# Half-megabyte clears between the key loads, one turn for a block's list loads, and new place numbers in an attention-and-experts kernel

## The chip, the cores and the metric

The kernel runs on one core of a Trainium2 chip. The metric is the time of one execution in device microseconds (us): lower is better. Five engines with instruction queues of their own work beside each other: TensorE (PE in the rows, its weight loads PEld), VectorE (DVE), ScalarE (ACT), GpSimd (POOL) and SyncE (SP). In this kernel SP computes nothing. It issues all plain transfers, one after the other, and POOL issues the gathers and scatters. TensorE runs at one of two clocks, 1.2 and 2.4 GHz; a granted clock of 1.00 in a stretch is the upper one throughout.

## What is computed

Attention of 8 batches with 8 heads, 576 rows, a causal window of 128 keys and a bias that falls with distance, and then a layer of 8 experts, of which every token takes two:

```python
scores = np.where(mask, scale * q @ k.T + slope * -abs(rel), -1e9)    # per batch and head
attn = np.exp(scores - scores.max(-1))                                # 576 x 576, window 128
x = ((attn / attn.sum(-1)) @ v)                                       # -> 4608 tokens x 512
noisy_logits = x @ w_gate + np.log1p(np.exp(x @ w_noise)) * noise     # 4608 x 8
top2 = the two largest of each row; top2_w = softmax over the two
for e in range(8):
    for k in range(2):
        mask = top2[:, k] == e
        h = np.maximum(x[mask] @ w1[e], 0.0)                          # 512 -> 1024
        out[mask] += top2_w[mask, k, None] * (h @ w2[e])              # 1024 -> 512
```

## The kernel before

**Attention and routing.** For each of 32 pairs (two heads of one batch) a key load brings queries and keys into one of five buffers (L465; batch b's values in two halves, L475). TensorE multiplies them (L524, L535), VectorE adds the bias and finds each row's largest (L539), ScalarE takes the exponentials (L563), TensorE transposes (L577, L581), ScalarE moves the result out of the accumulators (L276), and GpSimd cuts the window's ragged edge with two `affine_select` instructions (L600, L601). Only after these can TensorE weigh the values (L614, L623). At the end of a batch the result is turned row-major (L783 and VectorE L786), stored to the table `xs` in memory (L794, L797), and multiplied by the gate (L816, L827). `route` then picks the two experts of each token (noisy logits on POOL, L950 to L953, the largest by VectorE L885 and L889), counts ahead of each token how many earlier ones chose the same expert (L893 to L898) and writes the token numbers into per-expert lists (matmul L933, VectorE L941 and L942). A scatter on POOL adds these lists into the table `slots` in memory (L1009). The gates' weights go to `xs` by SP (L1069, L1073).

**The early blocks.** Batches are counted from b=0 to b=7. When b=3, b=5 and b=7 are through (`CUTS`), a block of expert 0's tokens is prepared, of 384, 384 and 256 rows, the first while attention still runs. For such a block, `first_ids` loads three (or two) pieces of the list from `slots` back by SP (L1078), VectorE turns them to indices (L1083, L1084, L1044), POOL gathers the rows of `xs` (L1337), VectorE splits them into 16-bit parts (L1434), and TensorE multiplies them by w1 (L1463) and w2 (L1613). Expert weights come by SP (L1321) and are split by VectorE (L1327).

**The second blocks.** Each expert then has two blocks of 512 rows (products L1489 and L1620) and one of what is left, 192 to 96 rows, whose first products (L1463) come as eight groups of twelve; each group's accumulator is emptied by ScalarE (L1588) and VectorE (L1603). Results are scattered into `out` by POOL (L1724), with addition. So `out` must be zero before the first of them: `set_ups` writes zeros to it and to the end of `xs` from a tile of zeros (L441), in ten transfers of 1 MB, and the tile then becomes a gather buffer.

**What sets the order.** The whole program is written as strands that a planner, the class `Order`, runs against a simple model of the five engines when the program is built. An operation has a duration in the model and a rank; an engine takes the waiting operation with the lowest rank, and buffers are handed out by rank as well. The ranks are sums of place numbers from the tables at the head of the file (`LOAD`, `VALUES`, `FINE`, `ROUTE`, `SCATTER` and so on) and of a batch's or a block's number. On TensorE an operation of the kind that ran last may go ahead if its rank is within `NEAR` of the best. The order that comes out is fixed: on the chip each engine runs its list in that order and waits wherever something is not there yet. A line `yield order.now + 2.5` tells the planner that a transfer takes so long to land; on the chip it is no wait, but it shifts what is issued when.

Two waits of the program matter here. The load of a list reads what the scatters wrote, and it waits for the landing of every scatter that stands ahead of it in the program, needed for this block or not. And the strand of `route` hands the table `slots` on from scatter to scatter through the ring `listing`, which the planner holds for the counted landing time only.

Of the kernel before, what the change touches and what calls it, by code (L numbers as in the profile page):

```python
# [13 lines left out]
AF = mybir.ActivationFunctionType  # L14
OP = mybir.AluOpType
AX = mybir.AxisListType
# [27 lines left out]
ZERO, EMPTY = -868.7, -2  # L44
LOAD = 1336.2
VALUES = 522.7
GATE = (586.3, 114.2, 10.8, 223.3, 430.5, 595.2, 1222.1, 914.0)
ROUTE = (342.7, 2091.0, 1245.6, 114.7, 453.4, 734.2, 1823.4, 1585.4)
SCATTER = (825.8, 1619.1, 1254.4, -2580.7, 356.1, -2057.0, -1202.6, 1165.8)
FFN0, FFN1 = -37.1, 674.3  # L50
WEIGHTS = (1547.8, 1129.9)
TOKENS = -408.2
FINE = (-269.6, -67.8, 591.7, 499.2, 364.6, 91.4, -84.0, -165.4, -508.6, -68.4, -409.6, 76.9, 124.7, -71.9, -108.9, -18.6, -921.6, 304.5, 493.5, 400.7, 136.3, 66.3, 526.5, 2.2, 234.2, -476.5, -453.8, -47.5, -184.4, -278.0, 410.0, 13.0, 37.2, 126.9, -246.8, 12.9, -248.7, 24.3, -130.2, 10.5, -211.1, 146.0, -91.2, -314.4, -30.9, 272.5, -306.7, -204.8, -795.2, 68.5, 336.3, -528.3, 344.2, 61.4, -456.9, 111.8, -186.5, -50.6, -10.3, -525.8, -189.2, 13.2, 55.1, 270.0, 177.0, -536.1, 113.3, 36.7, -51.7, -60.8, 589.7, -248.0, -73.3, -88.5, 652.2, -8.9, -517.4, 295.6, 24.0, -285.0, 895.7, 310.8, -678.8, -379.9, -384.9, -317.9, 31.8, 33.5, -239.2, -604.6, -100.3, -134.7, 154.5, -665.9, 43.3, 311.1, 207.6, -18.8, 338.4, -65.9, -144.2, -324.3, 36.8, 219.5, -55.9, -124.3, 200.0, -551.8, 229.5, 106.3, 1.0, 383.8, -156.7, -416.1, -291.1, -190.4, 45.4, -262.7, -141.2, 180.6, -150.6, -450.1, -201.8, 120.2, -203.1, -129.0, 273.6, 32.0, 96.8, -401.0, -263.6, 134.3, -151.3, 504.8, 21.3, -241.5, -6.7, -424.3, -701.9, 780.4, 28.0, 576.4, -208.7, 237.4, -534.3, 273.3, 215.7, 380.0, 228.8, -184.6, 104.7)
STAGE = (855.9, -105.9, 923.9, 172.5, -770.8, 1148.3, 1067.9, 742.9)
MIDDLE = 1144.0
RESULT = 1472.4
SIZES = (1334.5, 424.5, 1529.3)
SOON = -672.8
TIGHT = (1, 5, 7)
QUICK = (5, 7)  # L60
LATE = (2094.9, -890.9, 647.9, 1175.8, 179.1, -270.3, -892.6, -769.0, 507.2, -1321.9, -1248.3, -168.7, -2569.7, -1705.9, -1040.2)
LAG = 0.2
ADD, TWS = 0.34, 5
BEHIND = 11.7
# [3 lines left out]
PACE, READ_BY, AHEAD = 1.1, 2.0, 297.8  # L68
HELD = 3
SWITCH, NEAR = 0.093, 39.0  # L70
# [168 lines left out]
def attention_moe(ctx: ExitStack, tc: tile.TileContext, qk_, v, w_gate, w_noise, noise, w1, w2,  # L239
# [142 lines left out]
    def set_ups():  # L382
# [479 lines left out]
    def route(b):  # L862
# [156 lines left out]
        yield order.now + 2.5  # L1019
# [5 lines left out]
    def landed_list():  # L1025
        yield order.now + 2.1
        put(listing, 0)

    def first_ids(blk, cut, rank):
# [16 lines left out]
        yield dve(0.4, FINE[65] + rank, clipped)  # L1046
# [4 lines left out]
    def gates_out(b, rank, tp, d, oh, gg, gd, placed_):  # L1051

        G = nc.gpsimd
        yield pool(0.3, FINE[66] + rank, lambda: G.tensor_tensor(d[:, :, 0], tp[:, :, 1], tp[:, :, 0], op=OP.subtract))
# [982 lines left out]
```

## Time and profile before

| What | Value |
|---|---|
| runs shown, us | 1002.38, 1001.42, 998.83 |
| median of the runs, us | 1001.42 |
| the profiled execution's own time, us | 997.48 |
| its span in the trace, us | 995.7 |
| granted clock of TensorE, mean | 0.988 |
| TensorE busy, us (share of the span) | 951.8 (96%) |
| VectorE busy, us | 822.1 (83%) |
| ScalarE busy, us | 569.0 (57%) |
| GpSimd busy, us | 382.3 (38%) |
| transfers, MB | 188.89 |

The profiled execution is one run among others: its own time, 997.48 us, is 3.94 us below the median, and the span, 995.7 us, leaves 1.78 us outside the trace. All durations below are from this execution. The chain of waits that ended last is TensorE for the most part (40% of the span by engine, products L1620 and L1489 leading by line), and the idle time of the other engines matters only where TensorE ends up waiting for them. Attention takes the first 237 us, the experts the rest.

### The profile page before, as it was taken

How to read it: one execution, taken by the hardware profiler on the slowest of the kernel's cores; microseconds unless marked ns; L12 is line 12 of the kernel's file. 1: busy time of each engine (PE TensorE's matmuls, PEld its weight loads, DVE VectorE, ACT ScalarE, POOL GpSimd, SP SyncE). 2: the span in 40 equal slices, each digit the busy share in tenths (PEclk: the TensorE clock that was granted, in tenths of full speed). 3: DMA queues.
4: the chain of work that ended last, by engine and by line, in shares of the span. 5: the costliest groups of instructions: out<-in, count | busy, mean ns of one | idle time of the engine just before them, and what ended most of it. 6: DMA issues, size and time to landing. Idle time of an engine off the chain costs nothing. (4 is left out here: it accounts for less than half of the span.)

```text
span 995.7 us, 25350 instructions
## 1 busy us (share of the span) xinstructions
PE 951.8 (96%) x9040; PEld 668.4 (67%) x9040; DVE 822.1 (83%) x2813; ACT 569.0 (57%) x1516; POOL 382.3 (38%) x567
## 2 busy tenths in 40 slices
PE   7999899878999999999999999999999999999996
PEld 5777676655556967596768576766767586667753
DVE  8989899888558898797889988989897898889520
ACT  8998789751445656355646454654555374546312
POOL 4456567676333223222342234323313223343013
PEclk9999999988999999999999999999999999999998
DMA  9785688788799897797887688868997989686124
GB/s 327 241 270 184 182 261 245 215 259 215 206 256 213 216 220 151 167 180 210 163 218 172 164 166 222 192 188 132 224 179 188 200 195 242 114 174 133 19 33 52
DMA packets 236976, 188.89 MB, mean 190 GB/s; under 512 B 147696, under 2 KB 190992, under 8 KB 236848
## 3 DMA queue, kind: packets, MB, share of 16 engines
q1 hardware_dynamic: 219504, 148.31, 56.4%
q0 software_dynamic: 17344, 38.94, 21.4%
q8 instruction: 72, 1.18, 0.5%
q14 instruction: 56, 0.46, 0.1%
HBM read 116.24 MB, written 40.71 MB: 158 GB/s over the span
## 5 line engine op out<-in xcount | busy, mean ns | idle before, releaser
L1724 POOL DMA_INDIRECT out_dram<-yo,ix x69 | 123.7, 1793 | 255.1 <-ACT yo L276 178.3
L1620 PEld LDWEIGHTS <-hh 128*128 128x128 f16 x896 | 85.3, 98 | 73.3 <-issue 0.3
L1588 ACT ACTIVATE hh<-bank 128x256 f16<-128x256 f32 (+8 forms) x116 | 40.1, 347 | 142.3 <-PE bank L1463 57.8
L1620 PE MATMUL bank<-w2ha,hh 128*128 128x512 f16 x288 | 109.2, 379 | 0.0
L1620 PE MATMUL bank<-w2la,hh 128*128 128x512 f16 x288 | 109.2, 379 | 0.0
L1620 PE MATMUL bank<-w2ha,hl 128*128 128x512 f16 x288 | 109.2, 379 | 0.0
L1337 POOL DMA_INDIRECT xg<-xs_dram,ix x34 | 41.9, 1231 | 162.4 <-DVE ix L1084 103.2
L563 ACT ACTIVATE p<-p,nm 128x128 f32<-128x128 f32 x256 | 99.1, 394 | 4.2 <-DVE nm L539 4.0
L1489 PEld LDWEIGHTS <-wth 128*128 128x128 f16 x896 | 87.2, 98 | 18.4 <-issue 2.5
L1620 PEld LDWEIGHTS <-hl 128*128 128x128 f16 x448 | 43.8, 98 | 52.8
L1588 ACT ACTIVATE hh<-c 128x256 f16<-128x256 f32 (+1 forms) x82 | 41.6, 520 | 57.7 <-DVE c L1558 54.2
L524 PE MATMUL bank<-qk 64*64 64x192 f32 (+2 forms) x1152 | 61.4, 327 | 9.6 <-DVE nm L539 5.0
L539 DVE CUSTOM_DVE_ANT_0 p<-bank,bias 128x128 f32<-128x128 f32 x288 | 67.1, 285 | 1.4 <-PE bank L577 1.2
L614 PE MATMUL bank<-pT,vraw 128*64 128x128 f32 (+1 forms) x640 | 59.1, 332 | 8.3 <-POOL pT L601 3.8
L1603 DVE SCALAR_TENSOR_TENSOR hl<-bank,hh 128x384 f16<-128x384 f32 (+8 forms) x88 | 31.2, 363 | 42.1 <-ACT hh L1588 35.1
L276 ACT ACTIVATE yo<-bank,gw 128x512 f32<-128x512 f32 (+6 forms) x56 | 38.3, 686 | 46.5 <-PE bank L1620 22.2
L1337 POOL DMA_INDIRECT xp<-xs_dram,ix x35 | 42.1, 1204 | 58.3 <-DVE ix L1084 27.5
L1293 ACT ACTIVATE mraw<-mraw 128x1024 f32<-128x1024 f32 x56 | 58.6, 1048 | 7.4 <-DMA mraw<-in_w_dram 7.4
L1463 PEld LDWEIGHTS <-w1ha 128*128 128x128 f16 x544 | 48.7, 98 | 20.3 <-issue 0.6
L276 ACT ACTIVATE c<-bank 128x256 f32<-128x256 f32 x94 | 35.0, 378 | 47.2 <-PE bank L1489 46.6
L1489 PE MATMUL bank<-xhe,wth 128*128 128x256 f16 x224 | 61.0, 273 | 0.8 <-DVE c L1549 0.4
L1489 PE MATMUL bank<-xhw,wth 128*128 128x256 f16 x224 | 61.0, 272 | 0.6 <-DVE c L1549 0.4
(349 smaller groups left out, 3178.3 us busy)
## 6 DMA issues: line engine op xcount, KB each, us to landing
raw<-in_w_dram SPq DMA_DIRECT2D x144, 256.0 KB
mraw<-in_w_dram SPq DMA_DIRECT2D x56, 512.0 KB
qk<-in_qk_dram SPq DMA_DIRECT2D x32, 576.0 KB
vraw<-in_v_dram SPq DMA_DIRECT2D x16, 640.0 KB
out_dram<-xg SPq DMA_DIRECT2D x10, 1024.0 KB
xs_dram<-x SPq DMA_DIRECT2D x72, 128.0 KB
out_dram<-yo,ix POOLq DMA_INDIRECT x69
xs_dram<-xg SPq DMA_DIRECT2D x1, 1024.0 KB
```

What stands on the lines that cost most here:

```text
L276: nc.scalar.activation(o, i, AF.Copy, **kw)
L524: nc.tensor.matmul(s[h][r * 64:r * 64 + 64, o:o + n_ * 64], qk[half, m * 64:m * 64 + 64], blocks_of(qk[half, QW:QW + S], first_, step, n_) ...
L539: nc.vector.tensor_tensor_reduce(out=o, in0=i, in1=by, scale=-0.125, scalar=3.0e38, op0=OP.add, op1=OP.min, accum_out=m)
L563: nc.scalar.activation(pv, pv, AF.Exp, bias=nm[:, z, h:h + 1], scale=-1.0, accum_out=den[:, i, 2 * g + h:2 * g + h + 1])
L614: nc.tensor.matmul(y, t[:, kb, hh:hh + D], w, start=m == 0, stop=m == len(lst) - 1)
L1293: yield act(us, FINE[81] + rank, lambda: nc.scalar.activation(v, v, sum_, accum_out=o))
L1337: nc.gpsimd.indirect_dma_start(out=o, out_offset=None, in_=xs[0:blk.rows], in_offset=bass.IndirectOffsetOnAxis(ap=blk.at[0:r, j:j + 1], ax ...
L1463: nc.tensor.matmul(t[:, 0:blk.n], wp[:, c], x[:, c, 0:blk.n], start=c == 0 and z == 0, stop=c == 3 and z == 2)
L1489: nc.tensor.matmul(t, wp[:, at + kc], xp[:, 2 * o + kc], start=not add and kc + z == 0, stop=kc + z == 3, skip_group_check=add)
L1588: nc.scalar.activation(o, i, AF.Relu)
L1620: nc.tensor.matmul(blk.y[j], h[:, cs], wp, start=a == 0 and z + m == 0, stop=a == 3 and z + m == 3)
L1724: ins = nc.gpsimd.indirect_dma_start(out=out, out_offset=bass.IndirectOffsetOnAxis(ap=blk.ix[0:r, j:j + 1], axis=0), in_=t[0:r], in_offset ...
```

## The change

Four things are changed.

1. In `set_ups` each clear is halved: 22 transfers of 0.5 MB in place of eleven of 1 MB (ten for `out`, one for the end of `xs`). The first was released by the 31st of the 32 key loads and the others by the last (`EMPTY` -2); now the first is released by the sixth, the next by the seventh, and so on (`EMPTY` -27). `ZERO`, which lowers the rank from clear to clear, goes from -868.7 to -570.9 per piece.
2. In `route` the planner counts 4.8 us from a scatter to its landing, in place of 2.5 (what follows in the strand) and 2.1 (the ring `listing`).
3. `first_ids` takes the ring `listing` before its list loads and returns it when they are fetched. While it is held, no other scatter to `slots` is placed.
4. All place numbers are new.

```diff
-ZERO, EMPTY = -868.7, -2
-LOAD = 1336.2
+ZERO, EMPTY = -570.9, -27
+LOAD = 696.3
...
-BEHIND = 11.7
+BEHIND = 144.7
...
-SWITCH, NEAR = 0.093, 39.0
+SWITCH, NEAR = 0.093, 114.1
...
-        for z, (ap, r) in enumerate([(xs, N * XW)] + [(out, r * DM) for r in range(0, NPAD, 512)]):
-            row_ = 4 * DM + (0 if z else rest_)
+        parts_ = [(xs, N * XW, 4 * DM + rest_)] + [(out, r * DM, 4 * DM) for r in range(0, NPAD, 512)]
+        for z, (ap, at, row_) in enumerate((ap, at + 2 * DM * h, row_) for ap, at, row_ in parts_ for h in range(2)):
             yield loaded[min(PAIRS + EMPTY + z, PAIRS - 1)]
-            yield from move(9.6e5, 16 + ZERO * z, lambda ap=ap, r=r, row_=row_: nc.sync.dma_start(
-                dram(ap, r, [[row_, 128], [DM, 4], [1, DM]]), zero[:, None, :].to_broadcast([128, 4, DM])))
+            yield from move(4.8e5, 16 + ZERO * z, lambda ap=ap, at=at, row_=row_: nc.sync.dma_start(
+                dram(ap, at, [[row_, 128], [DM, 2], [1, DM]]), zero[:, None, :].to_broadcast([128, 2, DM])))
...
         yield sent[b]
         mark(routed[b])
         mark(over)
-        yield order.now + 2.5
+        yield order.now + 4.8
...
     def landed_list():
-        yield order.now + 2.1
+        yield order.now + 4.8
         put(listing, 0)
...
         for b in range(cut - 1):
             yield routed[b]
+        yield (listing, FINE[65] + rank)
         for j in range(nt):
             spawn(fetch_ids(ids[:, j], blk.s0 + j * 128, rank, fetched))
         yield fetched
+        put(listing, 0)
```

Two lines are added in `first_ids`, so that every later line number is larger by two in the changed kernel (the list load is L1078 before, L1080 after). The entries of `FINE` behind the new one move by one.

**SP, the issue of the first block's list loads.** `list` is the list of expert 0's tokens, `out_0` the output that is cleared, `qk` and `vraw` the key and value loads, `xs` the stores of attention's rows, `gd` those of the gates. Before:

```order
L441 DMA out_0_dram<-xg_125 512x1x512
L475 DMA vraw0_83<-in_v_dram 128x5x256
L1073 DMA xs_dram<-gd0_179 64x8
L1078 DMA list0_197<-slots_dram 128x1 x3
L441 DMA out_0_dram<-xg_125 512x1x512
L794 DMA xs_dram<-x2_113 64x512
L441 DMA out_0_dram<-xg_125 512x1x512
L475 DMA vraw1_84<-in_v_dram 128x5x256
```

After:

```order
L1071 DMA xs_dram<-gd0_179 64x4x8 x2
L797 DMA xs_dram<-x0_111 64x512 x2
L797 DMA xs_dram<-x1_112 64x512 x2
L1080 DMA list0_197<-slots_dram 128x1 x3
L441 DMA out_0_dram<-xg_125 128x2x512
L1075 DMA xs_dram<-gd0_179 64x8
L475 DMA vraw0_83<-in_v_dram 128x5x256
L441 DMA out_0_dram<-xg_125 128x2x512
L794 DMA xs_dram<-x2_113 64x512
L441 DMA out_0_dram<-xg_125 128x2x512
```

The clears stood behind the list loads for the most part: ahead of them SP had issued three of the eleven transfers, and eight (8 MB) came after. Now seventeen of the 22 (8.5 MB) are issued ahead, between the key loads from the sixth on, and five behind.

**POOL, the scatters of batches b=3 and b=4 and the first block's gathers.** `listed` holds a batch's lists, `cl` the first block's indices, `pT` the transposed exponentials. The scatter of b=3 stands some 15 rows further up in both programs. Before:

```order
L600 AFFINE_SELECT pTl0_100<-pTl0_100 128x2x128
L601 AFFINE_SELECT pTl0_100<-pTl0_100 128x2x128
L1008 MEMSET pad_131 1x1
L1009 DMA slots_dram<-listed0_180,line_of1_150 704x64
L600 AFFINE_SELECT pT1_99<-pT1_99 128x2x128
L601 AFFINE_SELECT pT1_99<-pT1_99 128x2x128
L600 AFFINE_SELECT pT1_99<-pT1_99 128x4x128
L601 AFFINE_SELECT pT1_99<-pT1_99 128x4x128
L1337 DMA xg_125<-xs_dram,cl0_199 128x520
```

After:

```order
L600 AFFINE_SELECT pT0_98<-pT0_98 128x4x128
L601 AFFINE_SELECT pT0_98<-pT0_98 128x4x128
L1339 DMA xg_125<-xs_dram,cl0_199 128x520
L1008 MEMSET pad_131 1x1
L1009 DMA slots_dram<-listed0_180,line_of1_150 704x64
L1339 DMA xg_125<-xs_dram,cl0_199 128x520
L1056 TENSOR_TENSOR d1_189<-tp1_184 128x5
L1339 DMA xg_125<-xs_dram,cl0_199 128x520
```

Before, the scatter of b=4 stood ahead of all three gathers, and (in the program) ahead of the list loads. After, the first gather comes before it. On VectorE the lists of b=3 end in row 896 before and 884 after, and the indices of the first block stand in row 986 before and 948 after, so that 64 rows lie between in place of 90. For the second block (its last batch is b=5) the two are rows 1068 and 1124 before, 1059 and 1091 after, and its gathers stand ahead of the scatter of b=6 now, behind it before.

**VectorE, the end of attention.** `th` are the parts of the gathered rows of the first early block, `w1l` and `w2l` the lower parts of the expert's weights, `l0` the noisy logits of a batch, `tp`, `idx` and `oh` its two largest. Before:

```order
L1434 SCALAR_TENSOR_TENSOR th_255<-xg_125,fit1_252,th_255 128x512
L1434 SCALAR_TENSOR_TENSOR th_255<-xg_125,fit2_253,th_255 128x512
L1327 SCALAR_TENSOR_TENSOR w2la4_225<-raw20_122,wsc_241,w2ha4_224 128x512
L1904 TENSOR_SCALAR gw0_243<-gw0_243,back_242 128x3
L1327 SCALAR_TENSOR_TENSOR w1la5_227<-raw11_120,wsc_241,w1ha5_226 128x512
L885 MAX tp0_168<-l0_167 128x8 x5
L1327 SCALAR_TENSOR_TENSOR w2la5_229<-raw21_123,wsc_241,w2ha5_228 128x512
L889 MAX_INDEX idx0_169<-tp0_168,l0_167 128x8 x5
L1327 SCALAR_TENSOR_TENSOR w1la6_231<-raw12_121,wsc_241,w1ha6_230 128x512
L957 TENSOR_TENSOR oh0_171<-idx0_169,names_142 128x80
L1327 SCALAR_TENSOR_TENSOR w2la6_233<-raw22_124,wsc_241,w2ha6_232 128x512
L959 TENSOR_TENSOR both0_172<-oh0_171 128x40
```

After:

```order
L1436 SCALAR_TENSOR_TENSOR th_255<-xg_125,fit1_252,th_255 128x512
L1436 SCALAR_TENSOR_TENSOR th_255<-xg_125,fit2_253,th_255 128x512
L1329 SCALAR_TENSOR_TENSOR w2la3_221<-raw22_124,wsc_241,w2ha3_220 128x512
L1906 TENSOR_SCALAR gw0_243<-gw0_243,back_242 128x3
L946 SCALAR_TENSOR_TENSOR l0_167<-lg0_161,l0_167 128x40
L1329 SCALAR_TENSOR_TENSOR w1la4_223<-raw10_119,wsc_241,w1ha4_222 128x512
L947 RECIPROCAL u0_166<-u0_166 128x40
L1329 SCALAR_TENSOR_TENSOR w2la4_225<-raw20_122,wsc_241,w2ha4_224 128x512
L1329 SCALAR_TENSOR_TENSOR w1la5_227<-raw11_120,wsc_241,w1ha5_226 128x512
L1329 SCALAR_TENSOR_TENSOR w2la5_229<-raw21_123,wsc_241,w2ha5_228 128x512
L885 MAX tp0_168<-l0_167 128x8 x5
L889 MAX_INDEX idx0_169<-tp0_168,l0_167 128x8 x5
```

The weight products and the row products were spread between the steps of the routing; now they stand in one run ahead of `MAX`. On POOL the scatter of b=5 now stands ahead of the two `affine_select` pairs of `pT0` and `pT1` that follow (it stood behind `pT0`'s).

**TensorE, the first products of an expert's last block.** `xh`, `xl` are the parts of the block's rows, `w1h`, `w1l` those of the weights, `hh` and `hl` those of the wide block's middle layer; each product has its weight load ahead of it. Before, at the first such place:

```order
L1463 LDWEIGHTS w1hb0_4579
L1463 MATMUL bank1_67<-xh0_4566,w1hb0_4579 128x192
L1463 LDWEIGHTS w1hb0_4579
L1463 MATMUL bank1_67<-xl0_4567,w1hb0_4579 128x192
L1463 LDWEIGHTS w1lb0_4580
L1463 MATMUL bank1_67<-xh0_4566,w1lb0_4580 128x192
L1620 LDWEIGHTS hh3_4568
L1620 MATMUL bank3_69<-w2ha0_208,hh3_4568 128x512
L1620 LDWEIGHTS hh3_4568
L1620 MATMUL bank3_69<-w2la0_209,hh3_4568 128x512
L1620 LDWEIGHTS hl3_4571
```

After:

```order
L1622 LDWEIGHTS hl2_261
L1622 MATMUL bank5_71<-w2ha3_220,hl2_261 128x512
L1465 LDWEIGHTS w1hb0_4589
L1465 MATMUL bank2_68<-xh0_4576,w1hb0_4589 128x192
L1465 LDWEIGHTS w1hb0_4589
L1465 MATMUL bank2_68<-xl0_4577,w1hb0_4589 128x192
L1465 LDWEIGHTS w1lb0_4590
L1465 MATMUL bank2_68<-xh0_4576,w1lb0_4590 128x192
```

Before, groups of three first products alternated with groups of six second products of the wide block: 33 of the 96 first products stood so, and 63 followed in a row. After, the 66 second products stand in a row, and nearly all 96 first products behind them, the eight groups of twelve back to back. It is so for the other experts too. The number of products of each kind is the same.

## Rows read from the trace of the kernel before

**Rows 1.** The page's first part: busy us, share of the span, instructions of each engine.

```profile
PE 951.8 (96%) x9040; PEld 668.4 (67%) x9040; DVE 822.1 (83%) x2813; ACT 569.0 (57%) x1516; POOL 382.3 (38%) x567
```

**Rows 2.** Stretches: length, PE, PEld, DVE, ACT, POOL busy, clock, DMA share, GB/s.

```profile
0.00:196.00 196.00, 178.16 (x2926) 131.72 (x2930) 181.16 (x1047) 170.24 (x712) 118.78 (x275) 0.99 0.77 245
196.00:201.00 5.00, 1.94 (x34) 1.22 (x28) 1.60 (x11) 2.57 (x11) 0.25 (x1) 0.89 0.35 122
201.00:217.00 16.00, 14.86 (x186) 10.82 (x186) 14.17 (x82) 11.48 (x39) 11.71 (x25) 0.82 0.88 273
217.00:231.00 14.00, 6.53 (x72) 4.42 (x73) 10.71 (x40) 3.18 (x9) 12.52 (x20) 0.76 0.77 194
237.00:986.00 749.00, 744.39 (x5758) 516.33 (x5755) 609.92 (x1618) 379.06 (x742) 237.31 (x246) 1.00 0.80 175
```

**Rows 3.** SP's waits, 150 to 260 us: total, times, longest.

```profile
SPq L1078 <- DMA slots_dram<-listed,line_of: 8.5, 2, 6.4
```

**Rows 4.** Timeline of SP: start, us, instruction.

```profile
188.90 1.32 SPq L1073 DMA_DIRECT2D xs_dram<-gd  x1
...
196.86 1.28 SPq L1078 DMA_DIRECT2D list<-slots_dram  x3
```

**Rows 5.** Timeline of POOL, in brackets the idle time before and its cause.

```profile
182.15 1.54 POOL L1009 DMA_INDIRECT slots_dram<-listed,line_of  x1 [0.18 <-issue]
...
190.95 1.44 POOL L1009 DMA_INDIRECT slots_dram<-listed,line_of  x1 [0.23 <-DVE rk L878]
...
200.75 1.01 POOL L1337 DMA_INDIRECT xg<-xs_dram,cl  x1 [6.16 <-DVE cl L1044]
```

**Rows 6.** Timeline of VectorE, the first block's indices.

```profile
199.91 0.16 DVE L1083 SCALAR_TENSOR_TENSOR ids<-list,spare 128x3 f32<-128x3 f32 x1 [3.33 <-DMA list<-slots_dram]
```

**Rows 7.** Timeline of TensorE, around the first block's list.

```profile
195.54 1.97 PE L524 MATMUL bank<-qk 64*64 64x192 f32 x36
...
201.13 1.11 PE L577 MATMUL bank<-ident,p 64*128 64x64 f32 x15 [3.19 <-DVE x L786]
202.17 3.25 PE L614 MATMUL bank<-pT,vraw 128*64 128x256 f32 x20
...
213.24 1.74 PE L614 MATMUL bank<-pT,vraw 128*64 128x256 f32 x20
214.91 0.71 PE L577 MATMUL bank<-ident,p 64*128 64x64 f32 x16
```

**Rows 8.** Timeline of TensorE, the end of attention and the first product behind it.

```profile
222.60 1.09 PE L614 MATMUL bank<-pT,vraw 128*64 128x256 f32 x12 [3.24 <-POOL pad L1008]
227.46 3.45 PE L614 MATMUL bank<-pT,vraw 128*64 128x256 f32 x20 [3.77 <-POOL pT L601]
...
236.72 0.33 PE L1463 MATMUL bank<-xhe,w1ha 128*128 128x384 f16 x1
```

**Rows 9.** Timeline of POOL at the first of these two waits.

```profile
219.34 0.63 POOL L600 TENSOR_SCALAR_AFFINE_SELECT pT<-pT 128x512 f32<-128x512 f32 x1
220.04 2.50 POOL L601 TENSOR_SCALAR_AFFINE_SELECT pT<-pT 128x512 f32<-128x512 f32 x1
```

**Rows 10.** Timeline of VectorE beside them.

```profile
220.06 1.31 DVE L1434 SCALAR_TENSOR_TENSOR th<-xg,fit,th 128x512 f16<-128x512 f32 x2
```

**Rows 11.** TensorE's waits, 0 to 240 us: total, times, longest.

```profile
PE bank L524 <- DMA qk<-in_qk_dram: 4.6, 1, 4.6
```

**Rows 12.** Two longer stretches, columns as in rows 2.

```profile
40.00:195.00 155.00, 143.50 (x2345) 105.44 (x2347) 144.84 (x824) 132.56 (x551) 100.82 (x220) 0.99 0.76 234
195.00:255.00 60.00, 47.07 (x511) 30.84 (x512) 48.62 (x227) 25.49 (x81) 35.30 (x65) 0.89 0.80 226
```

**Rows 13.** Tile view, clears of `out`: ns least/median/most, first and last start.

```profile
L441 SPq DMA_DIRECT2D out_dram<-xg x10: 569/596/606, 180.5 to 253.9; - x10
```

**Rows 14.** Timeline of SP, the last key load.

```profile
171.27 0.34 SPq L465 DMA_DIRECT2D qk<-in_qk_dram  x1
```

**Rows 15.** TensorE's waits, 237 to 987 us, one of nine kinds.

```profile
PE bank L1463 <- DVE hl L1603: 0.3, 1, 0.3
```

More of the change, by code (lines that the diff above doesn't have):

```diff
@@ L1184, in summed_weights @@
         for part in range(2):
-            yield dve(0.8, FINE[76] + rank, lambda part=part: sums_(nc.vector, part))
+            yield dve(0.8, FINE[77] + rank, lambda part=part: sums_(nc.vector, part))
         through_with(raw1, r0, uses0)
@@ L1341, in tokens @@
         if blk.wide:
-            blk.x = yield (xwr, FINE[89] + rank)
+            blk.x = yield (xwr, FINE[90] + rank)
             for q in range(2):
-                xp = yield (xpr, FINE[90] + rank)
+                xp = yield (xpr, FINE[91] + rank)
                 for i in range(2):
-                    yield pool(1.25, FINE[91] + rank, lambda: gather(q + 2 * i, 128, xp[:, i * XW:i * XW + XW]))
+                    yield pool(1.25, FINE[92] + rank, lambda: gather(q + 2 * i, 128, xp[:, i * XW:i * XW + XW]))
                 spawn(turn_pair(blk, q, xp, rank))
             return
-        blk.xh = yield (blk.rings["xh"], FINE[92] + rank)
-        blk.xl = yield (blk.rings["xl"], FINE[93] + rank)
+        blk.xh = yield (blk.rings["xh"], FINE[93] + rank)
+        blk.xl = yield (blk.rings["xl"], FINE[94] + rank)
         early = blk in first
         for j, r in blk.tiles:
-            xg = yield (xgr if early else xpr, FINE[94] + rank)
-            yield pool(1.25, FINE[95] + rank, lambda: gather(j, r, xg[0:r, 0:XW]))
+            xg = yield (xgr if early else xpr, FINE[95] + rank)
+            yield pool(1.25, FINE[96] + rank, lambda: gather(j, r, xg[0:r, 0:XW]))
             spawn(turn_tokens(blk, j, r, xg, rank))
@@ L1383, in sums_ @@
                 g.tensor_tensor(s4, a12, s2, op=OP.subtract)
-        hi, lo = yield (tpr, FINE[97] + rank)
+        hi, lo = yield (tpr, FINE[98] + rank)
         nothing_ = hi[:, 0:4 * HALF].rearrange("p (a b) -> p a b", a=2)
-        yield act(1.12, FINE[98] + rank, lambda: nc.scalar.activation(nothing_, rows, AF.Square, accum_out=big))
+        yield act(1.12, FINE[99] + rank, lambda: nc.scalar.activation(nothing_, rows, AF.Square, accum_out=big))
         for part in range(2):
-            yield dve(0.8, FINE[99] + rank, lambda part=part: sums_(nc.vector, part))
-        yield dve(1.16, FINE[100] + rank, powers)
+            yield dve(0.8, FINE[100] + rank, lambda part=part: sums_(nc.vector, part))
+        yield dve(1.16, FINE[101] + rank, powers)
         extra = xp[:, 2 * P:2 * P + 3 * HALF]
@@ L1638, in downs @@
                     for j in range(4):
-                        t = yield (yb, FINE[135] + rank)
+                        t = yield (yb, FINE[136] + rank)
                         blk.y.append(t)
                 for j, r in blk.tiles:
-                    end = yield pe(1.3, FINE[136] + rank, lambda: mm2_wide(blk, f, j, [ev[2] for ev in ws]), False)
+                    end = yield pe(1.3, FINE[137] + rank, lambda: mm2_wide(blk, f, j, [ev[2] for ev in ws]), False)
                     if f == 3:
@@ L1666, in downs @@
                 for c in range(4):
-                    end = yield pe(3 * (blk.n / 2400 + 0.005), FINE[139] + rank, lambda: mm2_flipped(blk, f, c, ev[2]), False)
+                    end = yield pe(3 * (blk.n / 2400 + 0.005), FINE[140] + rank, lambda: mm2_flipped(blk, f, c, ev[2]), False)
                     if f == 7:
@@ L1676, in downs @@
             for j, r in blk.tiles:
-                end = yield pe(0.655, FINE[140] + rank, lambda: mm2(blk, f, j, r, ev[2]), False)
+                end = yield pe(0.655, FINE[141] + rank, lambda: mm2(blk, f, j, r, ev[2]), False)
                 if f == 7:
@@ L1705, in turn @@
                 nc.tensor.transpose(a[0:r, c * 128:c * 128 + 128], blk.yt[c][:, j * 128:j * 128 + r], ident)
-        end = yield pe(0.43, FINE[144] + rank, turn, False)
+        end = yield pe(0.43, FINE[145] + rank, turn, False)
         if j == len(blk.tiles) - 1:
@@ L1861, in second_ids @@
     def second_ids():
-        yield order.now + 2.5
+        yield order.now + 4.8
         for q, blk in enumerate(second):
             rank = 1000 + 8 * q - AHEAD
-            t = blk.ix = blk.at = yield (ixr, FINE[148] + rank)
+            t = blk.ix = blk.at = yield (ixr, FINE[149] + rank)
             v = lists2[q % 2]
```

166 lines of the change are left out of this document (83 added, 83 removed).

## The prediction

> **What bounds the kernel now.** I read the stretches first, then the waits, then the timelines around the longest ones. TensorE is busy 951.8 us of the span [rows 1], and the stretches say where the rest lies [rows 2]: from 237 to 986 us it works 744.39 of 749 us at full clock, so at most 4.6 us can be won there, whatever the other engines do. The idle time is ahead of 237. Two places carry it. From 196 to 201 TensorE works 1.94 of 5.00 us, and from 217 to 231 it works 6.53 of 14.
>
> The first place is one chain. SP waits 6.4 us for the landing of a scatter before it may load the first block's list [rows 3]; the last thing it did was at 188.90, the list loads go out at 196.86 [rows 4]. The scatter it waits for is the one of b=4 at 190.95; the one of b=3, which alone the block needs, went out at 182.15 [rows 5]. VectorE stands at the indices for 3.33 us [rows 6], and behind them on VectorE stands the row-major work that TensorE needs: TensorE waits 3.19 us [rows 7]. POOL stands 6.16 us [rows 5].
>
> The second place: two waits of 3.24 and 3.77 us for POOL's window cuts [rows 8]. Ahead of the first, one cut took 2.50 us where its twin of the same form took 0.63 [rows 9], while VectorE ran products of two inputs [rows 10].
>
> **The change part by part.** The sum is made against the profiled execution, 997.48 us with a span of 995.7, which is 3.94 below the median of the runs shown, 1001.42.
>
> *List turn and longer landing.* With `listing` held, b=4's scatter stands behind the list loads, so SP waits for b=3's alone. Is its list there when VectorE comes to it? Issue to landing of the scatter is 196.86 - 190.95 = 5.9 us [rows 4, 5], list loads to indices 199.91 - 196.86 = 3.05 [rows 4, 6], and from the lists' last instruction to the scatter I allow 1 us, where the two scatters had stood 0.18 and 0.23 idle [rows 5]: 10 us. Between the lists and the indices VectorE now has 64 rows, 77 instructions; at 181.16 / 1047 = 0.173 us each [rows 2] that is 13.3 us. So the list is there 3 us early, and TensorE's 3.19 and VectorE's 3.33 go: **-3.3**. Bounds: 0, if something else on VectorE is late by as much; -6.2, POOL's whole wait. What is late next is the scatter of b=4, which stands behind the first gather on POOL: it could be held by up to a list's 3.05 us, but it has until the next block's list; 0, bounds 0 and +3. The longer counted landing is no wait on the chip; it lives in these places: 0.
>
> *The clock behind the wait.* Right behind the 3.19 us the same twenty products took 3.25 us against 1.74 later, and 15 transposes 1.11 against 0.71 for 16 [rows 7]; the granted clock of 201 to 217 is 0.82, between the lower level (1.2 GHz, 0.50) and the upper. That is 1.5 + 0.4 = 1.9 us. If the idle time goes, the fall should go with it, but TensorE may rest elsewhere: I take half, **-1.0** (0 to -1.9).
>
> *Clears.* 5.5 MB more are issued ahead of the list. From 40 to 195 us the transfers stood at a share of 0.76 with 234 GB/s [rows 12], thus some 308 GB/s at a full share: 5.5 MB take 17.9 us of the 155, and the share goes to 0.88. From 195 to 255 it falls from 0.80 by 17.9 / 60 = 0.30 to 0.50. SP has eleven issues more, at 0.596 us each [rows 13] 6.6 us of its 155. What hides this is the lead of the key loads: the last was issued at 171.27 [rows 14] and first used at 195.54 [rows 7], 24 us later. If that cover is gone, a key load costs what the first one cost, 4.6 us [rows 11]. I take 0, bounds -1 (the emptier stretch behind) and +4.6. The Trainium skill ("DMA: Bandwidth & Descriptors", section "Measured (HBM→SBUF, 128 partitions, SWDGE, issued from GpSimd)") asks for transfers of 1 MiB or more for three quarters of the peak, which speaks against halving the clears; at the 2 us of fixed time that its section "Anatomy of one DMA — SWDGE (gpsimd) path" states, eleven more would take 22 us (an estimate), and the sum would still be the same as long as keys arrive in time. It is stated for POOL's queue; the 308 GB/s here came from SP's transfers of 0.25 to 1 MB mixed.
>
> *New places, end of attention.* The waits of 3.24 and 3.77 are 7.0 us together [rows 8]. The scatter of b=5 moved ahead of two pairs of cuts, and VectorE's eight two-input products of 512 columns stand in one run ahead of `MAX`. Both ends are open: -7.0 if POOL is in time, and above, if the cuts are held through the run, 8 products of 1.31 / 2 = 0.655 us [rows 10] = 5.2, less the 2.50 - 0.63 = 1.87 that is lost now [rows 9]: +3.4. As nothing says that POOL has less to do there (12.52 of 14 us busy, [rows 2]), I stay near today's row: **-1.0**.
>
> *New places, second blocks.* The products are the same ones. Per expert 33 of 96 first products of the last block leave the company of second products: 33 / 12 = 2.75 groups, over seven experts 19. Behind a group TensorE needs an accumulator that VectorE has emptied. The one wait of this kind is 0.3 us [rows 15]; 19 of them are 5.8. But 63 / 12 x 7 = 36 groups ran back to back already, and all waits of the stretch together are 4.6 [rows 2], so the nearest row says almost nothing: 0. Bounds: -4.6 (every wait goes) and +5.8.
>
> Sum: -3.3 - 1.0 - 1.0 = -5.3. Run 997.48 - 5.3 = 992.2, and with the 3.94 between this run and the median **996.1 us**; the span would be 990.4.
>
> **The rivals.**
>
> *More goes (D).* POOL comes in time at the end as well: -3.3 - 1.0 - 7.0 = -11.3, 990.1. For it: the scatter no longer stands between the cuts, and the clears are gone from 195 to 255. Against: POOL is busy nine tenths of that stretch.
>
> *The cuts are held (C).* VectorE's run of eight products keeps POOL's cuts waiting: -3.3 - 1.0 + 3.4 = -0.9, 1000.5. For it: 2.50 against 0.63 with one pair of such products beside it. If the clock falls there too and the 1.0 is not won and the list is late after all, +3.4, 1004.8. The Trainium skill ("SBUF — State Buffer", section "Who interferes with whom") says that a VectorE instruction with two SBUF inputs contends with a GpSimd instruction that reads SBUF, and that whoever issues first holds the shared ports for the whole instruction. By that rule the order of the two decides, and by it the 1000.5 would stand wherever VectorE's run starts first. The trace's 2.50 us agrees, since 1.31 + 0.63 = 1.94 is most of it.
>
> *The change doesn't do what it says (E).* The list wait comes back, at this block or the next: there 32 rows lie between lists and indices where 55 lay. Then only the end's -1.0 is left: 1000.4. Against it: in those 32 rows stand the long products.
>
> *Keys come late (K), the slower one.* With transfers at 0.88 and 17 clears between key loads on one queue, a key load reaches TensorE late, and each time 4.6 us go [rows 11]. One leaves 1000.7. From two it decides: -5.3 + 9.2 = +3.9, 1005.3. For it: at a share of 0.88, in the stretch from 201 to 217, the queues moved 273 GB/s [rows 2], near all they gave anywhere. Against: 24 us of lead at the last.
>
> *The groups wait (B).* 19 x 0.3: -5.3 + 5.8 = +0.5, 1001.9; slower only from 0.43 us each (8.3 / 19). Against it are the 36 groups.
>
> **How the numbers follow.** A measurement of this kernel can tell some 0.3%, 3 us, from no change: faster is below 998.4, slower above 1004.4. Forecast 0.40 (its own range 992 to 998.4, all faster), D 0.16 (faster), C 0.17 (0.12 same, 0.05 slower), E 0.06 (same), K 0.12 (two key loads or more, slower), B 0.09 (0.05 same, 0.04 slower). Faster 0.40 + 0.16 = 0.56, same 0.12 + 0.06 + 0.05 = 0.23, slower 0.05 + 0.12 + 0.04 = 0.21. The range reaches from below D, with the list's -6.2 in place of -3.3 (987.2) and 2 us for runs that differ, to K's two key loads: 985 to 1006. Left out are a third key load and a worse B, and a larger gain, under 0.2 together.
>
> **What would show it.** Right: no wait of VectorE above 0.5 us at the list, POOL's first gather ahead of b=4's scatter, a granted clock near 1.00 from 200 to 210, the first product of the first block at about 231.4 in place of 236.72 [rows 8], 749 us from there to TensorE's end, a transfer share up to 0.88 from 40 to 195 and about 0.50 behind. Wrong: TensorE's waits for keys beyond the first 4.6 (K); cuts of 2 us and more at the end, with waits beyond 7.0 together (C); a second stretch longer than 752 us, with waits of L1465 for the emptied accumulator (B). If the list wait is gone and the first product still starts at 236, the gain was given back between the two places, and the step that failed is the end's -1.0.

## The result, and the profile after

| | before | after |
|---|---|---|
| median of the runs, us (runs) | 999.86 (5) | 990.32 (5) |
| lowest and highest, us | 998.63, 1002.38 | 989.08, 993.12 |
| profiled execution, its span, us | 997.48, 995.7 | 989.86, 988.1 |
| ratio, 95% interval | 1 | 0.9906 [0.9882, 0.9930] |

The change makes the kernel 0.9% faster. The two profiled executions differ by 7.6 us, the medians by 9.5. The median of the kernel before is over five runs here, three of them those of the first table, whose median was 1001.42.

The stretches of the kernel after, with the columns of [rows 2] and [rows 12]:

```profile
0.00:196.00 196.00, 181.96 (x2988) 133.82 (x2990) 184.81 (x1082) 172.66 (x713) 119.37 (x286) 0.99 0.88 284
196.00:201.00 5.00, 4.94 (x69) 3.05 (x63) 4.97 (x31) 5.00 (x19) 4.30 (x10) 1.00 0.66 184
201.00:217.00 16.00, 10.44 (x132) 7.84 (x132) 14.29 (x47) 8.98 (x33) 10.76 (x17) 0.89 0.67 153
217.00:231.00 14.00, 12.17 (x110) 7.76 (x107) 7.70 (x44) 3.01 (x7) 7.48 (x14) 0.64 0.65 185
237.00:978.00 741.00, 737.49 (x5710) 512.11 (x5708) 590.99 (x1577) 388.92 (x755) 228.41 (x233) 1.00 0.79 171
40.00:195.00 155.00, 147.32 (x2415) 107.49 (x2415) 148.63 (x860) 134.84 (x552) 100.54 (x228) 0.99 0.90 285
195.00:255.00 60.00, 52.21 (x480) 32.81 (x481) 48.85 (x212) 27.03 (x85) 31.51 (x61) 0.89 0.51 122
```

The hole from 196 to 201 is gone: 4.94 us of work in 5.00, where it was 1.94. But TensorE had already 3.8 us more work behind it at 196 (181.96 against 178.16), and no step of the prediction speaks of that stretch. The list comes as forecast; these are the rows of POOL, SP and VectorE in the kernel after, in the order of time:

```profile
169.74 1.51 POOL L1009 DMA_INDIRECT slots_dram<-listed,line_of  x1 [0.28 <-DVE bank L555]
```

```profile
179.09 2.21 SPq L1080 DMA_DIRECT2D list<-slots_dram  x3
```

```profile
183.42 0.16 DVE L1085 SCALAR_TENSOR_TENSOR ids<-list,spare 128x3 f32<-128x3 f32 x1
...
183.81 0.17 DVE L1046 TENSOR_SCALAR cl<-ids 128x3 int32<-128x3 int32 x1
```

```profile
184.25 1.02 POOL L1339 DMA_INDIRECT xg<-xs_dram,cl  x1 [1.53 <-DMA out_dram<-xg]
...
185.58 1.48 POOL L1009 DMA_INDIRECT slots_dram<-listed,line_of  x1 [0.23 <-DVE bank L545]
```

No wait stands in brackets at the indices, where 3.33 us stood [rows 6]. The scatter of b=4 (185.58) follows the first gather.

The stretch that the prediction passed over shows itself on POOL. First the kernel before, from 90 to 104 us: the scatter of b=0, that of b=1, and the gate sums behind it.

```profile
92.34 1.68 POOL L1009 DMA_INDIRECT slots_dram<-listed,line_of  x1 [0.33 <-DVE nm L539]
...
99.43 1.46 POOL L1009 DMA_INDIRECT slots_dram<-listed,line_of  x1 [5.37 <-DVE bank L545]
100.37 1.81 POOL L841 TENSOR_TENSOR lt<-lt 128x256 f32<-128x256 f32 x2
102.26 0.32 POOL L842 TENSOR_TENSOR lg<-lt 128x64 f32<-128x64 f32 x1
```

And TensorE of the kernel before, behind it:

```profile
104.26 1.05 PE L783 MATMUL bank<-ident,xul 128*64 128x128 f32 x4 [2.67 <-ACT pT L276]
```

POOL of the kernel after, at the same two scatters:

```profile
92.89 1.68 POOL L1009 DMA_INDIRECT slots_dram<-listed,line_of  x1 [0.20 <-issue]
94.10 1.16 POOL L841 TENSOR_TENSOR lt<-lt 64x64 f32<-64x64 f32 x2
...
99.78 1.46 POOL L1009 DMA_INDIRECT slots_dram<-listed,line_of  x1 [0.43 <-DMA slots_dram<-listed,line_of]
```

Both times some 7 us lie between the starts of the two scatters, since the second adds to the table that the first is still writing. Before, POOL stood 5.37 us of them and the gate sums stood behind it. The profile names VectorE as what ended the wait, but the lists that this scatter adds were done at 96.53 (L942), 2.9 us earlier, and the kernel after names the transfer itself. After, POOL works through ten rows in the meantime and stands 0.43.

The end of attention, TensorE of the kernel after:

```profile
201.56 1.74 PE L614 MATMUL bank<-pT,vraw 128*64 128x256 f32 x20
...
211.96 0.87 PE L614 MATMUL bank<-pT,vraw 128*64 128x256 f32 x8 [1.61 <-POOL pT L601]
215.48 1.97 PE L614 MATMUL bank<-pT,vraw 128*64 128x256 f32 x12 [2.65 <-POOL pT L601]
218.24 3.26 PE L614 MATMUL bank<-pT,vraw 128*64 128x256 f32 x20 [0.79 <-ACT xu L276]
...
230.14 0.33 PE L1465 MATMUL bank<-xhe,w1ha 128*128 128x384 f16 x1
```

POOL's cuts still keep TensorE waiting, 1.61 + 2.65 = 4.26 us in place of the 7.0 of [rows 8]; with the 0.79 that is put down to ScalarE it is 5.05. The first product of the first block stands at 230.14 in place of 236.72: 6.6 us earlier. Ahead of that product TensorE stood idle 236.72 - 206.84 = 29.9 us before and 230.14 - 208.66 = 21.5 after; 1.8 us of the 8.4 come back as more busy time (granted clock 0.64 from 217 to 231, where it was 0.76; over the whole way to the first product it is 0.96 in both kernels). From that product to TensorE's end it took 749.6 us before and 748.6 after.

### The profile page after: what moved, and what is told of

Same layout as the page of the kernel before. It is cut to its first block, busy times and chain, and to the rows that moved or that the text cites. A ratio compares the mean times of both kernels' runs of the same rounds, so it can differ in the third digit from the quotient of the medians.

```text
span 988.1 us, 25335 instructions
## 1 busy us (share of the span) xinstructions
PE 953.4 (96%) x9040; PEld 668.3 (68%) x9040; DVE 808.5 (82%) x2792; ACT 583.1 (59%) x1537; POOL 375.2 (38%) x567
## 5 line engine op out<-in xcount | busy, mean ns | idle before, releaser
L1726 POOL DMA_INDIRECT out_dram<-yo,ix x69 | 125.9, 1824 | 242.7 <-ACT yo L276 174.9
L1622 PEld LDWEIGHTS <-hh 128*128 128x128 f16 x896 | 87.3, 98 | 86.6 <-issue 0.6
L1339 POOL DMA_INDIRECT xp<-xs_dram,ix x35 | 47.6, 1360 | 186.8 <-DVE ix L1086 116.7
L276 ACT ACTIVATE yo<-bank,gw 128x512 f32<-128x512 f32 (+5 forms) x60 | 41.0, 687 | 86.9 <-PE bank L1622 43.5
L1590 ACT ACTIVATE hh<-c 128x256 f16<-128x256 f32 (+1 forms) x92 | 46.3, 517 | 61.7 <-DVE c L1560 59.8
L614 PE MATMUL bank<-pT,vraw 128*64 128x128 f32 (+1 forms) x640 | 58.7, 330 | 8.5 <-POOL pT L601 4.7
L1622 PE MATMUL bank<-w2hb,hh 128*128 128x512 f16 x160 | 60.6, 379 | 0.5 <-ACT yt L276 0.5
L1491 PE MATMUL bank<-xhw,wtl 128*128 128x256 f16 x224 | 61.1, 273 | 0.0
L1491 PE MATMUL bank<-xlw,wth 128*128 128x256 f16 x224 | 61.1, 273 | 0.0
L1491 PE MATMUL bank<-xhe,wtl 128*128 128x256 f16 x224 | 61.0, 272 | 0.0
```

Source lines behind the costliest of these rows:

```text
L276: nc.scalar.activation(o, i, AF.Copy, **kw)
L614: nc.tensor.matmul(y, t[:, kb, hh:hh + D], w, start=m == 0, stop=m == len(lst) - 1)
L1339: nc.gpsimd.indirect_dma_start(out=o, out_offset=None, in_=xs[0:blk.rows], in_offset=bass.IndirectOffsetOnAxis(ap=blk.at[0:r, j:j + 1], ax ...
L1491: nc.tensor.matmul(t, wp[:, at + kc], xp[:, 2 * o + kc], start=not add and kc + z == 0, stop=kc + z == 3, skip_group_check=add)
L1590: nc.scalar.activation(o, i, AF.Relu)
L1622: nc.tensor.matmul(blk.y[j], h[:, cs], wp, start=a == 0 and z + m == 0, stop=a == 3 and z + m == 3)
```

## Experiments

Ratios are against the kernel before on the same chip, with 95% intervals. Except where the text says that the planner sets the order anew, its work is untouched: an instruction is only handed out later or earlier, and all other rows of all engines stand as they stood. Added lines shift the line numbers (with six, L1009 is L1015 and L614 is L620). In the first of the edits `HOLD = {b: n}` issues the scatter of batch b behind the next n operations of POOL:

```diff
             what.emit(e) if len(what.on) > 1 else what.emit()
+            if e == "POOL":
+                for h in self.held:
+                    h[0] -= 1
+                while self.held and self.held[0][0] <= 0:
+                    self.held.pop(0)[1]()
...
+    HOLD = {1: 5}
+    def held_(scatter, b):
+        return (lambda: order.held.append([HOLD[b] + 1, scatter])) if b in HOLD else scatter
-        yield pool(1.2, FINE[64] + rank, scatter)
+        yield pool(1.2, FINE[64] + rank, held_(scatter, b))
```

**The scatter of b=1 alone** (`HOLD = {1: 5}` in the kernel before).

> The kernel before with one scatter moved: b=1's scatter to slots is issued five POOL operations later (behind two gate sums, two pairs of cuts and the ranks), as far from b=0's as the changed kernel has it; all other rows stand as before. Theory S (the gain ahead of 196 us comes from POOL no longer standing 5.37 us at 99.43 for the landing of b=0's scatter): TensorE's wait of 2.67 at 104.26 and the low clock behind it go, about 3 to 4 us less, 0.9960 to 0.9970 of before. Rival P (VectorE, 181 of 196 us busy, sets attention's pace, and the new place numbers gave the gain elsewhere): the wait turns up again later, less than 1 us, 0.999 to 1.000.

Measured: 0.9978 [0.9962, 0.9993], 2.2 us less. POOL's wait for the landing is gone (its rows in this kernel, then one of TensorE):

```profile
92.51 1.67 POOL L1015 DMA_INDIRECT slots_dram<-listed,line_of  x1 [0.33 <-DVE nm L545]
97.40 1.26 POOL L847 TENSOR_TENSOR lt<-lt 128x256 f32<-128x256 f32 x2 [3.22 <-DVE lt L838]
...
104.52 1.53 POOL L1015 DMA_INDIRECT slots_dram<-listed,line_of  x1 [0.18 <-issue]
```

```profile
101.64 0.63 PE L789 MATMUL bank<-ident,xul 128*64 128x128 f32 x4
```

POOL still stands, 3.22 us for VectorE, so 5.37 us was not the price of the landing alone; but the gate sums start at 97.40 in place of 100.37, 3.0 us earlier. TensorE's row that waited 2.67 us starts without a wait, 2.6 us earlier. In the profiled execution the first product of the first block comes at 232.99, 3.7 us earlier, and TensorE ends 3.4 us earlier. The mechanism of theory S is what the rows show; the gain over all runs lies between its 3 to 4 us and the less than 1 of rival P, and its interval, 0.7 to 3.8 us, reaches into both.

**The scatter of b=4 alone** (`HOLD = {4: 3}`).

> The kernel before with one scatter moved: b=4's scatter is issued three POOL operations later, behind the first gather of block 0 and so behind its list loads; all other rows stand as before. Theory S: SP no longer waits 6.4 us for it, TensorE's 3.19 us at 201.13 go and part of the 1.9 us of low clock, 3.3 to 5 us less, 0.9950 to 0.9967. Rival P: the waits of 7.0 us at the end of attention take it back, under 1 us, 0.999 to 1.000. Rival W: POOL waits for the list in front of the first gather and the scatter of b=4 comes late, up to 3 us slower, 1.003.

Measured: 0.9985 [0.9972, 0.9998], 1.5 us less, below theory S's 3.3 to 5 and above rival P's 1. The wait at the list is gone, and the first product comes at 232.83, 3.9 us earlier. In the profiled execution most of this is lost at one place later: TensorE waits for ScalarE, and ScalarE for a weight load. First the wait of TensorE, then ScalarE's rows:

```profile
281.68 0.39 PE L1623 MATMUL bank<-w2ha,hh 128*128 128x512 f16 x1 [2.31 <-ACT hh L1598]
```

```profile
280.10 1.06 ACT L1303 ACTIVATE mraw<-mraw 128x1024 f32<-128x1024 f32 x1 [7.60 <-DMA mraw<-in_w_dram]
...
281.15 0.47 ACT L1598 ACTIVATE hh<-bank 128x384 f16<-128x384 f32 x1
```

So the stall's price is as forecast where it stands, and this execution gives most of it back. That it is given back because TensorE comes earlier is not shown: with both scatters moved (next), TensorE comes to the same product earlier still, and the only wait of its that the profile lists there, from 236 to 320 us, is 0.4 for VectorE. Rival W falls.

**Both** (`HOLD = {1: 5, 4: 3}`).

> The kernel before with both scatters moved, b=1's by five and b=4's by three POOL operations. Theory S: both gains add up, 6 to 9 us less, 0.991 to 0.994, which is all that the change gave. Rival P: 1 to 2 us less, 0.998, and the rest of the change's 9.5 us is in the other places.

Measured: 0.9951 [0.9936, 0.9966], 4.9 us less: about half of the change, and between what theory S and rival P expected. The two gains add up (2.2 + 1.5, and the intervals allow 4.9), and no later wait takes them; the rest of the change is elsewhere.

**The clears early, alone.**

```diff
+    WITH = {5 + round(z * 26 / 16): z for z in range(17)}
...
+        def key():
+            nc.sync.dma_start(t, dram(qk_, k * 128 * (QW + S), [[QW + S, 128], [1, QW + S]]))
+            if k in WITH:
+                piece(WITH[k])     # half a megabyte of zeros
```

> The kernel before with the clears alone moved: 17 half-megabyte pieces are issued right behind key loads from the sixth to the last, the other five stand where clears stood before behind the list loads; the rows of all other engines stand as before. Prediction's term: 0 (between -1 and +1), share of the transfers from 40 to 195 us up from 0.76 to 0.88, no new key wait. Rival K: a key load comes late twice or more, 4.6 us each, 1.005 or more. Rival C (the emptier stretch from 195 to 255 shortens the end of attention): 1 to 3 us less, 0.997 to 0.999.

Measured: 0.9999 [0.9983, 1.0016]. The sum is 0, but of two parts. The second scatter of the pair waits longer (POOL), and TensorE behind it:

```profile
94.07 1.68 POOL L1020 DMA_INDIRECT slots_dram<-listed,line_of  x1 [0.33 <-DVE nm L550]
102.77 1.46 POOL L1020 DMA_INDIRECT slots_dram<-listed,line_of  x1 [6.98 <-DVE x L797]
```

```profile
107.61 1.06 PE L794 MATMUL bank<-ident,xul 128*64 128x128 f32 x4 [4.33 <-ACT pT L276]
```

TensorE's wait is 4.33 in place of 2.67. At the first block's list it waits 1.3 in place of 3.19, since SP waits for that landing 4.5 in place of 6.4. No key came late. The transfers' share from 40 to 195 us came to 0.82, not to the 0.88 expected.

**The same program again.** In the changed kernel only `landed_list` is put back to 2.1.

> The changed kernel with the counted landing in front of the next turn on slots put back from 4.8 to 2.1 us. The planner makes row for row the order of the changed kernel from it, on all five engines. So every theory expects the changed kernel's time, 0.9906 of before within 0.002; it tells how far apart two takes of one program are. If it is near 0.995, the change's gain was read too large, and two scatters moved in the kernel before (0.9951) explain all of it.

Measured: 990.46 us, 0.9912 [0.9892, 0.9933]. The changed kernel's time repeats. Its profile does so less closely: the first product stands at 231.34 here and at 230.14 in the changed kernel's own, the same order, so a difference of about 1 us between two profiled executions says nothing. The order says more than the time: under the new place numbers this number changes no row. If the turn itself (`yield (listing, ...)` and its `put`) is taken out of the changed kernel, the planner moves one row on VectorE by one place and nothing else; the time of that kernel is not known. So what set b=4's scatter behind the list loads in the changed kernel is not the turn.

**The pair of scatters brought back** (`HOLD = {0: 5}` in the changed kernel).

> The changed kernel with one scatter moved back: b=0's is issued five POOL operations later, so that it stands right ahead of b=1's, as in the kernel before; all other rows as in the changed kernel. Theory S (POOL stands for the first one's landing, and what is queued behind it makes TensorE wait): 2 to 4 us slower than the changed kernel, 0.9926 to 0.9946 of before. Rival P (it cost nothing of itself): 0.9906.

Measured: 993.12 us, 0.9942 [0.9920, 0.9964], 2.7 us more than the same program without it. The converse of the first experiment, with about the same size in time, though the landing came sooner: the first scatter starts at 99.73 here, 4.4 us ahead of the second, and POOL stands 2.66. POOL's row of the second scatter:

```profile
104.12 1.46 POOL L1015 DMA_INDIRECT slots_dram<-listed,line_of  x1 [2.66 <-DMA slots_dram<-listed,line_of]
```

**The clears late in the changed order.**

```diff
+        WHEN = [[]] * 11 + [[z] for z in range(11, 17)] + [[0, 1, 17], [2, 3, 18], [4, 5, 19], [6, 7, 20], [8, 9, 10, 21]]
...
+            late_.append(lambda ap=ap, at=at, row_=row_: nc.sync.dma_start(...))
+            yield from move(4.8e5, 16 + ZERO * z, lambda z=z: [late_[x]() for x in WHEN[z]])
```

> The changed kernel with eleven of the half-megabyte clears (5.5 MB) held back: they are issued with the last five, behind the first block's list loads, so that 3 MB go ahead of these and 8 MB behind, as before; all other rows as in the changed kernel. Prediction's term: 0 (between -1 and +1 us). Theory E (moved alone in the kernel before, the early clears lost 4 us up to 104 us and won 3.5 between 104 and 205; in the changed order nothing waits for a scatter at 100, so only the win is left): 2 to 4 us slower than the changed kernel, 0.9926 to 0.9946 of before.

Measured: 990.29 us, 0.9909 [0.9889, 0.9930]. No difference, though the share of the transfers from 195 to 255 us is 0.70, against 0.51 in the changed kernel. Theory E falls: the emptier stretch is worth nothing that shows here, to some 2 us, and the prediction's 0 holds.

**Both scatters and the clears in the kernel before.**

> The kernel before with both scatters moved and the clears early, all other rows as before. If the clears are worth nothing: 0.995, as with both scatters alone (0.9951). Theory E: 2 to 3.5 us more, 0.9915 to 0.993, and the new places are worth little (0.9906 with them). If the clears slow something else in this order too: 0.996 or more, and the places are worth 4 us or more.

Measured: 995.37 us, 0.9956 [0.9937, 0.9975]; with both scatters alone it was 0.9951. The clears add nothing, and what is left to the changed kernel's 0.991 belongs to the new order.

**The three parts without the numbers, and the numbers without the parts.** Here the planner sets the order anew.

> The kernel before with all three parts of the change that are not place numbers (half-megabyte clears from the sixth key load on, the list loads in the turn of slots, 4.8 us counted for a landing), under the old place numbers; the planner sets the order anew from them. In it the two first scatters stand 8 rows of POOL apart and the scatter of b=4 behind the first gather. Theory S (the distance between scatters and what reads or follows them is what counts): 0.992 to 0.995. Rival P (the numbers themselves, which fit the places to these parts, are needed): 0.997 to 1.003, since places fitted to other parts cost something elsewhere.

> The changed kernel with the three other parts put back as before (1 MB clears behind the last key loads, no turn, 2.5 and 2.1 us counted), so with the new place numbers alone; the planner sets the order anew. Its first two scatters stand 12 rows of POOL apart and the scatter of b=4 stands 46 rows behind the last gather of the first block. Theory S: near the changed kernel, 0.990 to 0.994. Rival P (numbers and parts only work together): 0.996 to 1.003.

Measured: the parts alone 997.34 us, 0.9997 [0.9979, 1.0016]; the numbers alone 1001.79 us, 1.0022 [1.0003, 1.0041]. Rival P holds. With the parts alone the list wait is gone and the waits for POOL's cuts are a little shorter, 5.8 us in place of 7.0, yet the first product starts at 236.9, no earlier than before. What eats it are smaller waits ahead: from 120 to 196 us TensorE works 68.3 us, where it worked 70.0 in the kernel before, and it waits more often for VectorE's row maxima (5.0 us in nine waits before). TensorE's waits of that kernel from 10 to 240 us, total, times, longest:

```profile
PE bank L524 <- DVE nm L539: 6.3, 13, 1.1
PE bank L614 <- POOL pT L601: 5.8, 3, 4.6
```

With the numbers alone the first product starts at 232.2, and the experts lose it again: TensorE's waits from 240 to 1005 us:

```profile
PE bank L1463 <- DVE hl L1603: 9.4, 6, 2.8
PE bank L1489 <- DVE c L1558: 3.2, 1, 3.2
```

That is the rival B of the prediction, in its place (the back-to-back groups of the last blocks) and at 1.6 us a wait. The size is that of a long execution: the profiled one took 1010.07 us, the most of twelve, 8.3 above their median, so part of these waits may be its own. The changed kernel has the same groups and, from 300 to 990 us, these waits:

```profile
PE bank L1491 <- DVE c L1560: 1.7, 3, 1.2
PE bank L1465 <- DVE hl L1605: 1.0, 3, 0.5
```

**The scatter of b=5 behind the cuts**, in the changed kernel (`HOLD = {5: 1}`, then `{5: 3}`).

> The changed kernel with the scatter of b=5 one POOL operation later, behind the first pair of cuts; all other rows the same. In the changed kernel TensorE waits 1.61 us for these cuts while POOL spends 1.75 us on the scatter ahead of them. If POOL's queue sets the end of attention: 1 to 1.6 us less, 0.9892 to 0.9900. If the cuts are slow because of VectorE's products beside them: the time is lost in the next cuts, 0.9905 to 0.9912.

> The same with the scatter of b=5 three POOL operations later, behind both pairs of cuts and the ranks between them. If POOL's queue sets the end of attention: 2 to 3 us less than the changed kernel, 0.988 to 0.989, unless the list of the second block, about 6 us later, makes VectorE wait at its indices (then 0.991 to 0.994). If the cuts are held by VectorE: 0.9905 to 0.9912.

Measured: 985.62 us, 0.9868 [0.9845, 0.9892], and 986.46 us, 0.9879 [0.9856, 0.9901]. Both are faster than the kernel before; against the changed kernel the difference is 4 to 5 us by medians, measured at another time, and the intervals overlap at their edges (up to 0.9892 and 0.9901 here, from 0.9882 and 0.9892 for the changed kernel and its repeat). TensorE with the scatter one operation later:

```profile
210.05 0.87 PE L620 MATMUL bank<-pT,vraw 128*64 128x256 f32 x8
215.18 1.98 PE L620 MATMUL bank<-pT,vraw 128*64 128x256 f32 x12 [4.26 <-POOL pT L607]
```

The first wait of 1.61 is gone and the second has grown from 2.65 to 4.26, the sum of both: in the profiled execution the end of attention is no shorter by it. The first product stands at 229.2 (230.14), and 2 us more are won among the experts, whose rows are the same. So the time of the first is better than either reading of the waits allowed, and why is not settled; the second came out as the reading by POOL's queue had it, but as the first did no worse, the two together do not show that POOL's queue is the cause.

## Why the prediction held, and which of its steps did not

The time, 990.32 us, lies within 985 to 1006, on the side that was forecast, but below the forecast's own range of 992 to 998.4: the gain is larger than the 5.3 us of the sum. It is the time of rival D (990.1) without D's mechanism, since 4.26 of the 7.0 us of waits at the end remain; that the two numbers meet is chance. Point by point:

- **The list wait, -3.3 and -1.0 for the clock.** The mechanism of the wait held: 14.3 us passed on VectorE between lists and indices (169.12 to 183.42; 13.3 forecast), no wait, the clock 1.00 from 196 to 201, twenty products in 1.74 us where they took 3.25 [rows 7]. The clock's -1.0 did not stay won: the low clock stands at the end of attention instead (twenty products in 3.26 us at 218.24), and TensorE's busy time up to the first product is 1.8 us more, not 1.0 less. What named the cause failed: "with `listing` held, b=4's scatter stands behind the list loads" is not why; under the new numbers it stands there without the turn. In the old order this move gave 1.5 us alone, with 3.9 us won at the first product, of which the profiled execution lost most later.
- **Longer landing, 0, and no term for the places ahead of 196.** Here is the step that failed. The sum prices the new places at the end of attention and in the second blocks, and of the scatters it follows b=4's only. The same distance counts between any two scatters to `slots`, and POOL's 5.37 us at 99 us stood in the trace of before, with the two scatters next to each other in the order. Moving them apart measured -2.2 in the old order, and bringing them together +2.7 in the new one. The counted landing itself is not what moved them in the changed kernel: put back to 2.1 it changes no row, and with the numbers alone the two stand 12 rows apart; the new numbers do it. With this term in the sum, -5.3 - 2.2 = -7.5, and the profiled executions differ by 7.6; that the two agree so well is partly chance, since the list and the clock gave less and the end more.
- **Clears, 0.** Held in both orders (0.9999, and 0.9909 against 0.9912, each to some 2 us). In the changed order no key came late, as the prediction had it; in the old order the 0 was the sum of a longer wait between scatters and a shorter one at the list, neither of which it priced. The shares came out at 0.90 and 0.51 (0.88 and 0.50 forecast). The halves cost nothing that shows: 285 GB/s at a share of 0.90, a little above the 308 x 0.90 = 277 that the old mix gave. The Trainium skill ("DMA: Bandwidth & Descriptors", section "Measured (HBM→SBUF, 128 partitions, SWDGE, issued from GpSimd)") asks for 1 MiB or more; on SP's transfers here the measurement shows no loss at half of it.
- **End of attention, -1.0.** 7.0 us of waits became 5.05, so -2.0, and the low clock (0.64 from 217 to 231) stayed. The cuts are still slowed while VectorE's run goes on (POOL of the kernel after; the forms take 0.41 and 0.64 undisturbed):

```profile
209.79 1.29 POOL L600 TENSOR_SCALAR_AFFINE_SELECT pT<-pT 128x256 f32<-128x256 f32 x1
211.16 0.75 POOL L601 TENSOR_SCALAR_AFFINE_SELECT pT<-pT 128x256 f32<-128x256 f32 x1
...
213.18 1.20 POOL L600 TENSOR_SCALAR_AFFINE_SELECT pT<-pT 128x512 f32<-128x512 f32 x1
214.45 0.98 POOL L601 TENSOR_SCALAR_AFFINE_SELECT pT<-pT 128x512 f32<-128x512 f32 x1
```

  That is 2.1 us over these four, spread, where 1.87 fell on one before. The rival C has its mechanism and not its price. The Trainium skill ("SBUF — State Buffer", section "Who interferes with whom") has one instruction hold the other for its whole length; the 0.88 us lost by the first of the four is about one product of 0.65 to 0.85 us. The rows do not test which instruction holds which: VectorE's products beside the last two of these cuts took 1.13 and 1.12 us in place of 0.65, so both engines lose there. The prediction's word that the trace agrees goes too far for the same reason: in [rows 9] and [rows 10] the slow cut starts at 220.04, ahead of VectorE's pair at 220.06, and by that rule it would have gone first.
- **Experts, 0.** 749.6 and 748.6 us. Rival B shows where the numbers stand without the parts, and hardly in the changed kernel (1.0 us in three waits).

What stays open: the two moved scatters and the clears explain 0.995 to 0.996 of the old order, the changed kernel has 0.991. The rest came with the new numbers and the parts together and was not taken apart; its cause stays open. The profiled executions show where some of it may lie: from the first product of the first block to that of the third it took 62.1 us before and 60.8 after, and TensorE's waits for VectorE's row maxima, 0 to 240 us, total, times, longest, are in the kernel before

```profile
PE bank L524 <- DVE nm L539: 5.0, 9, 1.0
```

and in the kernel after

```profile
PE bank L524 <- DVE nm L539: 2.1, 6, 0.6
```


## What to carry to other kernels

Where two transfers write one table, look for every place where a second one follows closely in an in-order queue, not only for the one that bounds the critical path today: what is queued behind it pays. Before crediting a new wait or lock with an order, take it out and compare the orders; here the numbers had made it idle. And place numbers fitted to a program are part of it: parts and numbers each alone were worth nothing or less, together 0.9%.

## What the runs showed of the hardware

- A scatter to a table that another scatter is still writing started some 7 us after the first one's start (92.34 to 99.43, 92.89 to 99.78), 8.7 us (94.07 to 102.77) with half-megabyte clears between the key loads of the old order, and 4.4 us (99.73 to 104.12) where the pair was brought back into the new one. What sets the length is not shown.
- A wait that the profile puts down to VectorE (99.43, before) was the transfer's to its end: the same wait, nearly over when POOL comes to it, is put down to the transfer (0.43, after).
- Executions of one program spread: 992.79 to 1001.94 us in 23 runs of the kernel before; of the changed order 989.08 to 993.12 in five runs and 990.10 to 991.17 in six.
